# Packed attention with two MoE feed-forward layers: the first two decode steps of the first layer's weight tiles are kept in program order

## The chip, the cores and the metric

The kernel runs on one core of a Trainium2 chip. The metric is the device time of one execution in microseconds (us). It is measured by running the compiled program several times. One more execution is recorded by the hardware profiler, and the rows below come from that one.

## The reference

```python
def _attn_ref(q, k, v, p):                       # q, k, v: (4, 8, 576, 64); p: (4, 8, 32, 64)
    scale = 1.0 / np.sqrt(q.shape[-1])
    def sm_attn(qq, kk, vv):
        s = scale * np.matmul(qq, kk.transpose(0, 1, 3, 2))
        a = np.exp(s - np.max(s, axis=-1, keepdims=True))
        a = a / (np.sum(a, axis=-1, keepdims=True) + 1e-09)
        return np.matmul(a, vv)
    p_packed = sm_attn(p, k, v)                  # 32 packed tokens a head
    return sm_attn(q, p_packed, p_packed)

def _moe_ref(x, w_in, w_out):                    # x: (2304, 512); w_in: (512, 2048)
    h = x @ w_in
    sp = np.where(h > 20.0, h, np.log1p(np.exp(np.minimum(h, 20.0))))
    return (h * np.tanh(sp)) @ w_out             # mish

def _moe2_ref(x, w_in, w_out):                   # the same shapes, with ELU
    h = x @ w_in
    g = np.where(h > 0.0, h, np.exp(np.minimum(h, 0.0)) - 1.0)
    return g @ w_out
```

The attention's result is laid out as 2304 tokens by 512 and goes through the mish layer (the first mixture) and then the ELU layer (the second mixture). The weights of the two mixtures are float64 in the inputs, and the kernel reads them as pairs of 32-bit words.

## The kernel before

The work is three stages that overlap. **Attention** runs by batch b (four batches). Keys and queries are transposed on VectorE (DVE, L261). `scores1` multiplies the packed tokens with the keys on TensorE (PE, L281); DVE takes the row maxima (L295, L296) and ScalarE (ACT) the exponential (L301). `scores2` multiplies queries with the packed result (PE, L391). DVE transposes what comes out (L405), takes the maximum (L412), subtracts it (L413), sums (L418 to L420), normalises (L421) and transposes back (L428), with the exponential on ACT (L414). The result is split into a high and a low part, `a2h` (ACT, L192) and `a2l` (DVE, L194).

**The first mixture** is written as a loop over n. `gemm1(n)` is six matmuls (L484 to L486) into a tile `h1` of PSUM; there are two such tiles, so group n + 2 waits until `mish` has read group n. `mish(n)` is ACT L493 and L494 and DVE L495. `gemm2(n)` is twelve matmuls (L512 to L514) and follows two groups behind. The w_in weights are not used as they are: `fold(b, c)` (PE, L453) first multiplies them with the packed attention of batch b, and ACT and DVE split the product into `gh` and `gl` (L192, L196). So `gemm1` needs `a2h`, `a2l` of its batch, and `gh`, `gl` of its batch and of its quarter c of the columns.

**The second mixture** is `gemm3` and `gemm4`, with weights that were decoded under the first mixture.

A weight tile of 128 rows by 512 values comes as 128 by 1024 words by a DMA (L126) and is decoded in five steps:

- s0: ACT rescales the exponent word in place (L159)
- s1: DVE shifts and masks it (L163)
- s2: DVE adds the sign (L169)
- s3: DVE adds the bits of the other word (L174)
- s4: the tile is split into high and low (ACT L192, then DVE L196), or, for w_in of the first mixture, stored for a later reload

The first mixture has 32 such tiles, here called i0..i3 of quarter c (`raw_w1i<r>_<c>`) and o0..o15 (`raw_w1o<r>`). The table `ORD` gives their order: i0 to i3 of c = 0, o0, then i0, i2, i1, i3 of c = 1, then o2, o3, o1, o4, o5, o6, o7, then c = 2. One half of `w1oh0` is tile o0 and the other is o1: `gemm2(0)` uses the first and `gemm2(1)` the second. `startup` traces the attention of batch 0 from a list and puts decode steps between its items; the list's items are under a raised priority, the decode steps are not.

The order on each engine is not the traced one. A scheduler with a timeline model picks, instruction by instruction, what stands next on each engine. A call of `tc.keep_in_program_order(ins)` fixes an instruction behind everything that was traced ahead of it on its engine. Before the change `pin` in `decode` makes that call for s0 and s1 of the second mixture's tiles (names `w2...`) and not for the first mixture's.

Of the kernel before, what the change touches and what calls it, by code (L numbers as in the profile page):

```python
# [43 lines left out]
def kernel(  # L44
# [39 lines left out]
    def slot(shape, dt, name):  # L84
        return up.tile(shape, dt, tag="u", name=name)
# [49 lines left out]
    def decode(name, r, c, staged=False):  # L135
        raw = raws.pop((name, r, c))
        rr = raw.rearrange("p (n two) -> p n two", two=2)
        w0, w1 = rr[:, :, 0], rr[:, :, 1]
        t = dp.tile([128, 512], I32, tag="dec", name="dec")
        f1 = w1.bitcast(F32)  # L140
        whole = name == "w1i"
        key = {"w1i": (c, r // 2), "w2i": (name, c, r // 2)}.get(name, (name, r // 2))
        if staged:
            if r % 2 == 0:
                w2_dr[key] = dr.tile([128, 2, 2, 512], F32, name=f"w2_dr{name}{r}_{c}")
            parts = raw.bitcast(F32R).rearrange("p (x n) -> p x n", x=2)
        elif r % 2 == 0:
            if whole:
                w1v[key] = slot([128, 2, 512], F32, f"w1v{c}_{r}")
            else:  # L150
                wt[key] = [(small if name == "w2o" and r >= 12 else slot)([128, 2, 512], F32R, f"{name}{x}{r}_{c}") for x in "hl"]
        oi = w1v[key][:, r % 2, :].bitcast(I32) if whole else t

        def pin(ins):
            if name[1] == "2":
                tc.keep_in_program_order(ins)

        def s0():
            pin(nc.scalar.activation(out=f1, in_=f1, func=ACTF.Copy, scale=REBIAS))  # L159

        def s1():
            pin(
                nc.vector.tensor_scalar(  # L163
                    out=t, in0=w1, scalar1=3, scalar2=0x7FFFFFF8, op0=ALU.logical_shift_left, op1=ALU.bitwise_and
                )
            )

        def s2():
            nc.vector.scalar_tensor_tensor(  # L169
                out=t, in0=w1, scalar=-0x80000000, in1=t, op0=ALU.bitwise_and, op1=ALU.bitwise_or  # L170
            )

        def s3():
            nc.vector.scalar_tensor_tensor(  # L174
                out=oi, in0=w0, scalar=29, in1=t, op0=ALU.logical_shift_right, op1=ALU.bitwise_or
            )

        def s4():
            if whole:
                if r % 2 == 1:  # L180
                    nc.gpsimd.dma_start(out=w1_dr[c * 2 + r // 2], in_=w1v[key])
            elif staged:
                split(t.bitcast(F32), parts[:, 0], parts[:, 1], 1.0 / WSCALE)
                nc.gpsimd.dma_start(out=w2_dr[key][:, r % 2], in_=parts.bitcast(F32))
            else:
                hi, lo = wt[key]
                split(t.bitcast(F32), hi[:, r % 2, :], lo[:, r % 2, :], 1.0 / WSCALE)

        return [s0, s1, s2, s3, s4]

    def split(val, hi, lo, factor=1.0):
        nc.scalar.activation(out=hi, in_=val, func=ACTF.Copy, scale=factor)  # L192
        if factor == 1.0:
            nc.vector.tensor_tensor(out=lo, in0=val, in1=hi.bitcast(F32), op=ALU.subtract)  # L194
        else:
            nc.vector.scalar_tensor_tensor(  # L196
                out=lo, in0=val, scalar=factor, in1=hi.bitcast(F32), op0=ALU.mult, op1=ALU.subtract
            )
# [683 lines left out]
```

## Time and profile before

| | us |
|---|---|
| median of three runs | 835.19 (833.59 to 835.94) |
| the profiled execution, its own time | 833.58 |
| its span, first to last instruction | 831.8 |
| busy in the span: PE, DVE, ACT | 768.9, 442.3, 345.0 |
| granted TensorE clock, mean over the span | 0.96 |

The span is what the rows below lie in; 1.8 us of the profiled execution's time lie outside it. A busy share is an average over the whole span: PE is at 92%, but with a start in which it mostly waits and a long rest in which it does not. The granted clock is a share of 2.4 GHz, so 1.00 is 2.4 GHz and 0.50 is 1.2 GHz.

### The profile page before, as it was taken

How to read it: one execution, taken by the hardware profiler on the slowest of the kernel's cores; microseconds unless marked ns; L12 is line 12 of the kernel's file. 1: busy time of each engine (PE TensorE's matmuls, PEld its weight loads, DVE VectorE, ACT ScalarE, POOL GpSimd, SP SyncE). 2: the span in 40 equal slices, each digit the busy share in tenths (PEclk: the TensorE clock that was granted, in tenths of full speed). 3: DMA queues.
4: the chain of work that ended last, by engine and by line, in shares of the span. 5: the costliest groups of instructions: out<-in, count | busy, mean ns of one | idle time of the engine just before them, and what ended most of it. 6: DMA issues, size and time to landing. Idle time of an engine off the chain costs nothing.

```text
span 831.8 us, 13033 instructions
## 1 busy us (share of the span) xinstructions
PE 768.9 (92%) x5172; PEld 665.2 (80%) x5172; DVE 442.3 (53%) x860; ACT 345.0 (41%) x672; POOL 23.0 (3%) x46
## 2 busy tenths in 40 slices
PE   4404998999999999999999999999999999999997
PEld 3204896979989898899998888888888888888886
DVE  2689877585677557773516753513243334342342
ACT  0356673557466656564524442312241223221222
POOL 0000000000100001000000000000000000000000
PEclk7556999999999999999999999999999999999999
DMA  8996177227756576431492410200020001000000
GB/s 190 260 413 244 67 249 184 97 78 226 191 216 223 184 183 220 156 105 62 144 365 81 127 51 23 79 1 0 1 77 13 0 1 51 13 1 1 26 26 25
DMA packets 92700, 96.79 MB, mean 116 GB/s; under 512 B 64224, under 2 KB 68832, under 8 KB 92640
## 3 DMA queue, kind: packets, MB, share of 16 engines
q1 hardware_dynamic: 81056, 77.55, 30.3%
q0 software_dynamic: 4736, 17.30, 5.3%
q10 hardware_dynamic: 6848, 1.11, 0.8%
q8 instruction: 40, 0.66, 0.3%
q14 instruction: 20, 0.16, 0.1%
HBM read 73.92 MB, written 22.02 MB: 115 GB/s over the span
## 4 chain that ended last, share of the span: by engine, by line
PE 85%; DMA 6%; DVE 3%; ACT 2%; SPq 2%; issue 1%; ACTq 0%; DVEq 0%
PE h L576 8%; PE h L574 8%; PE h L575 8%; PE o L597 8%; PE o L598 8%; PE o L599 8%; PE acc L513 7%; PE acc L514 7%; PE acc L512 7%; PE h L484 4%; PE h L485 4%; PE h L486 4%; PE pm L453 1%; DMA raw_w1o<-in_moe_w_out_dram 1%; DMA k<-in_k_dram 1%
## 5 line engine op out<-in xcount | busy, mean ns | idle before, releaser
L513 PE MATMUL acc<-gl,w1oh 128*128 128x288 f32 x512 | 151.1, 297 | 0.1
L514 PE MATMUL acc<-gh,w1ol 128*128 128x288 f32 x512 | 150.6, 296 | 0.0
L512 PE MATMUL acc<-gh,w1oh 128*128 128x288 f32 x512 | 147.1, 296 | 0.0
L575 PE MATMUL h<-yl,w2ih 128*128 128x512 f32 (+1 forms) x320 | 117.7, 368 | 0.0
L576 PE MATMUL h<-yh,w2il 128*128 128x512 f32 (+1 forms) x320 | 117.5, 368 | 0.0
L574 PE MATMUL h<-yh,w2ih 128*128 128x512 f32 (+1 forms) x320 | 116.7, 368 | 0.0
L597 PE MATMUL o<-w2oh,gh 128*128 128x512 f32 x288 | 112.4, 390 | 1.1 <-ACT ob L249 0.7
L598 PE MATMUL o<-w2ol,gh 128*128 128x512 f32 x288 | 112.2, 390 | 0.0
L578 ACT ACTIVATE t<-h 128x512 f32<-128x512 f32 (+1 forms) x80 | 42.9, 554 | 166.1 <-PE h L576 151.5
L599 PE MATMUL o<-w2oh,gl 128*128 128x512 f32 x288 | 108.3, 389 | 0.0
L579 DVE TENSOR_SCALAR t<-t 128x512 f32<-128x512 f32 (+1 forms) x80 | 31.7, 399 | 143.0 <-ACT t L578 142.3
L513 PEld LDWEIGHTS acc<-gl,w1oh 128*128 128x128 f32 x512 | 96.3, 188 | 7.6 <-issue 3.8
L495 DVE TENSOR_TENSOR gl<-t,gh 128x288 fp32r<-128x288 f32 x128 | 57.8, 453 | 81.2 <-ACT gh L494 80.4
L514 PEld LDWEIGHTS acc<-gh,w1ol 128*128 128x128 f32 x512 | 96.3, 188 | 2.9 <-issue 2.7
L512 PEld LDWEIGHTS acc<-gh,w1oh 128*128 128x128 f32 x512 | 95.2, 189 | 4.1 <-DVE y L251 1.7
L484 PE MATMUL h<-a2h,gh 128*128 128x288 f32 x256 | 77.6, 304 | 14.7 <-ACT a2h L192 12.0
L493 ACT ACTIVATE t<-h 128x288 f32<-128x288 f32 x128 | 52.1, 408 | 88.4 <-PE h L486 86.0
L485 PE MATMUL h<-a2l,gh 128*128 128x288 f32 x256 | 76.9, 301 | 2.5 <-DVE a2l L194 2.5
L192 ACT ACTIVATE gh<-t 128x512 fp32r<-128x512 f32 (+1 forms) x80 | 46.6, 588 | 78.4 <-DVE t L580 49.3
L486 PE MATMUL h<-a2h,gl 128*128 128x288 f32 x256 | 76.8, 300 | 0.6 <-DVE gl L196 0.5
L194 DVE TENSOR_TENSOR gl<-t,gh 128x512 fp32r<-128x512 f32 (+1 forms) x80 | 50.2, 637 | 40.9 <-ACT gh L192 39.5
L576 PEld LDWEIGHTS h<-yh,w2il 128*128 128x128 f32 x320 | 60.2, 188 | 10.3
(102 smaller groups left out, 1103.6 us busy)
## 6 DMA issues: line engine op xcount, KB each, us to landing
w1r<-w_dr SPq DMA_DIRECT2D x24, 512.0 KB, 5.4
raw_w2i<-in_moe_w_in_dram SPq DMA_DIRECT2D x16, 512.0 KB, 4.1
raw_w1i<-in_moe_w_in_dram SPq DMA_DIRECT2D x16, 512.0 KB, 6.4
raw_w1o<-in_moe_w_out_dram SPq DMA_DIRECT2D x16, 512.0 KB, 10.9
raw_w2o<-in_moe_w_out_dram SPq DMA_DIRECT2D x16, 512.0 KB, 3.7
k<-in_k_dram SPq DMA_DIRECT2D x16, 288.0 KB, 6.6
y_dr<-y POOLq DMA_DIRECT2D x16, 288.0 KB, 2.6
out_dram<-ob SPq DMA_DIRECT2D x18, 256.0 KB, 2.0
```

The lines of the kernel that those rows point to most:

```text
L484: nc.tensor.matmul(out=hp, lhsT=wh, rhs=xh, start=(kt == 0), stop=False)
L485: nc.tensor.matmul(out=hp, lhsT=wh, rhs=xl, start=False, stop=False)
L486: nc.tensor.matmul(out=hp, lhsT=wl, rhs=xh, start=False, stop=(kt == 1))
L512: nc.tensor.matmul(out=o, lhsT=wh[:, cs], rhs=gh, start=first, stop=False)
L513: nc.tensor.matmul(out=o, lhsT=wh[:, cs], rhs=gl, start=False, stop=False)
L514: nc.tensor.matmul(out=o, lhsT=wl[:, cs], rhs=gh, start=False, stop=last)
L574: nc.tensor.matmul(out=hp, lhsT=wh, rhs=xh, start=(i == 0), stop=False)
L575: nc.tensor.matmul(out=hp, lhsT=wh, rhs=xl, start=False, stop=False)
L576: nc.tensor.matmul(out=hp, lhsT=wl, rhs=xh, start=False, stop=(i == 3))
L597: nc.tensor.matmul(out=o, lhsT=gh[:, ts], rhs=wh, start=(kk == 0), stop=False)
L598: nc.tensor.matmul(out=o, lhsT=gh[:, ts], rhs=wl, start=False, stop=False)
L599: nc.tensor.matmul(out=o, lhsT=gl[:, ts], rhs=wh, start=False, stop=(kk == NK - 1))
```

## The change

```diff
         def pin(ins):
-            if name[1] == "2":
-                tc.keep_in_program_order(ins)
+            tc.keep_in_program_order(ins)
 
         def s0():
             pin(nc.scalar.activation(out=f1, in_=f1, func=ACTF.Copy, scale=REBIAS))
```

`pin` is called in s0 and s1 alone. The call is now made for the 32 tiles of the first mixture too: 32 instructions L159 on ACT and 32 instructions L163 on DVE now stand behind everything that was traced ahead of them on their engine. No instruction is computed differently. Lines behind the diff carry numbers that are one lower in the changed kernel (L404 there is L405 here).

What this does to the order is read from the two built programs. First DVE, from the last query transpose of batch 0 on (`qT0_3`; `x0_*` and `pm_369`, `pm_382` belong to `scores2` of batch 0; `dec_457`, `dec_465`, `dec_473` are tiles i0, i2, i1 of c = 1; `gl0_0` is the low part of `fold(0, 0)`; `dec_446`/`w1ol0_0` are tile o0). Before:

```order
L261 STREAM_TRANSPOSE qT0_3_367<-q0_3_194 128x576
L174 SCALAR_TENSOR_TENSOR dec_446<-raw_w1o0_0_187,dec_446 128x512
L163 TENSOR_SCALAR dec_457<-raw_w1i0_1_199 128x512
L169 SCALAR_TENSOR_TENSOR dec_457<-raw_w1i0_1_199,dec_457 128x512
L163 TENSOR_SCALAR dec_465<-raw_w1i2_1_201 128x512
L169 SCALAR_TENSOR_TENSOR dec_465<-raw_w1i2_1_201,dec_465 128x512
L196 SCALAR_TENSOR_TENSOR gl0_0_421<-pm_411,gh0_0_420 128x512
L196 SCALAR_TENSOR_TENSOR w1ol0_0_448<-dec_446,w1oh0_0_447 128x512
L174 SCALAR_TENSOR_TENSOR w1v1_0_458<-raw_w1i0_1_199,dec_457 128x512
L174 SCALAR_TENSOR_TENSOR w1v1_2_466<-raw_w1i2_1_201,dec_465 128x512
L163 TENSOR_SCALAR dec_473<-raw_w1i1_1_203 128x512
L196 SCALAR_TENSOR_TENSOR gl0_0_421<-pm_411,gh0_0_420 128x512
L405 STREAM_TRANSPOSE x0_0_378<-pm_369 128x288
```

And in the changed kernel:

```order
L260 STREAM_TRANSPOSE qT0_3_367<-q0_3_194 128x576
L404 STREAM_TRANSPOSE x0_0_378<-pm_369 128x288
L404 STREAM_TRANSPOSE x0_1_380<-pm_369 128x288
L404 STREAM_TRANSPOSE x0_0_378<-pm_382 128x288
L404 STREAM_TRANSPOSE x0_1_380<-pm_382 128x288
L411 TENSOR_REDUCE mx2_393<-x0_0_378 128x18
```

Eleven decode and split instructions stood between the query transpose and the first L405; now none does. They follow behind the last instruction of the chain of batch 0 (`a2l0`), with tile o0 first.

Second ACT, around the exponential of `scores1` for batch 1, its first half (`e1_1_0`, which reads the maximum `sm_838`). `t1_726`, `t1_759`, `t1_792`, `t1_852` are `mish` of n = 6, 7, 8, 9. Before, with o11 the last of the decode steps ahead of it:

```order
L493 ACTIVATE t1_792<-h1_785 128x288
L494 ACTIVATE gh1_793<-t1_792 128x288
L192 ACTIVATE w1oh8_0_801<-dec_860 128x512
L493 ACTIVATE t1_852<-h1_845 128x288
L159 ACTIVATE raw_w1o11_0_858<-raw_w1o11_0_858 128x512
L301 ACT_TABLE_LOAD
L301 ACTIVATE e1_1_0_842,sm_838<-pm_821,sm_838 128x9x32 x2
L494 ACTIVATE gh1_853<-t1_852 128x288
```

And in the changed kernel:

```order
L493 ACTIVATE gh1_700<-t1_699 128x288
L191 ACTIVATE w1oh6_0_582<-dec_603 128x512
L300 ACT_TABLE_LOAD
L300 ACTIVATE e1_1_0_842,sm_838<-pm_821,sm_838 128x9x32 x2
L492 ACT_TABLE_LOAD
L492 ACTIVATE t1_726<-h1_719 128x288
L493 ACTIVATE gh1_727<-t1_726 128x288
```

The exponential and the two table loads around it stood behind `mish` of n = 9; now they stand ahead of `mish` of n = 6.

Third PE. `h1_538` is `gemm1(0)`, `pm_529` is `fold(0, 1)`, which needs `w1v1` (the four tiles i of c = 1). Before:

```order
L391 MATMUL pm_382<-qT0_0_361,pt_323 32x288 x2
L453 MATMUL pm_529<-w1v1_2_466,pt_323 32x512 x4
L453 MATMUL pm_529<-w1v1_0_458,pt_323 32x512 x4
L484 MATMUL h1_538<-a2h0_431,gh0_0_420 128x288
```

In the changed kernel the fold stands behind `gemm1(0)` to `gemm1(3)` and `gemm2(0)`, whose last matmul is the first row here, and ahead of `gemm2(1)`, which reads the half of `w1oh0` that is tile o1:

```order
L512 MATMUL acc1_611<-gl1_547,w1oh0_0_447 128x288
L513 MATMUL acc1_611<-gh1_546,w1ol0_0_448 128x288
L452 MATMUL pm_529<-w1v1_2_466,pt_323 32x512 x4
L452 MATMUL pm_529<-w1v1_0_458,pt_323 32x512 x4
L511 MATMUL acc0_610<-gh1_576,w1oh0_0_447 128x288
```

Up to the first matmul of `gemm1(8)` (`h1_785`) both programs hold the same 268 matmul instructions on PE, in a different order. On SP, the queue that issues the loads, the four loads of batch 1's keys stood behind the load of o9 and now stand ahead of the load of o5, and the loads of batch 1's values move ahead of the reload of `w1v` and of tile i0 of c = 3. In the second mixture only neighbouring rows change places.

## Rows read from the trace of the kernel before

**Rows 1.** The page: the span and its instructions.

```profile
span 831.8 us, 13033 instructions
```

**Rows 2.** Stretches: length, busy PE, PEld, DVE, ACT, POOL, granted clock, DMA share, GB/s.

```profile
80.00:90.00 10.00, 10.00 (x99) 9.19 (x98) 10.00 (x21) 3.81 (x9) 0.77 (x1) 1.00 0.42 119
101.00:103.20 2.20, 0.63 (x25) 0.10 (x9) 2.20 (x6) 2.14 (x5) 0.00 (x0) 1.00 0.23 54
127.00:130.00 3.00, 1.70 (x50) 1.06 (x58) 1.34 (x5) 0.71 (x2) 0.00 (x0) 0.94 0.70 115
130.00:133.00 3.00, 3.00 (x22) 1.48 (x7) 1.90 (x4) 1.30 (x3) 0.00 (x0) 0.50 0.58 92
150.00:790.00 640.00, 639.08 (x4073) 556.25 (x4072) 319.02 (x600) 264.11 (x507) 17.36 (x32) 1.00 0.30 96
```

**Rows 3.** Timeline of PE: start, length, instruction, [idle before, its releaser].

```profile
39.75 1.88 PE L391 MATMUL pm<-qT,pt 64*32 64x288 f32 x32
...
73.93 0.61 PE L485 MATMUL h<-a2l,gh 128*128 128x288 f32 x1 [2.47 <-DVE a2l L194]
...
93.95 0.29 PE L484 MATMUL h<-a2h,gh 128*128 128x288 f32 x1
...
103.16 0.40 PE L484 MATMUL h<-a2h,gh 128*128 128x288 f32 x1 [1.57 <-ACT t L493]
```

**Rows 4.** Timeline of DVE.

```profile
38.07 0.78 DVE L261 STREAM_TRANSPOSE qT<-q 128x576 f32<-128x576 f32 x1
...
42.01 0.43 DVE L163 TENSOR_SCALAR dec<-raw_w1i 128x512 int32<-128x512 int32 x1 [2.59 <-ACT raw_w1i L159]
42.48 0.69 DVE L169 SCALAR_TENSOR_TENSOR dec<-raw_w1i,dec 128x512 int32<-128x512 int32 x1
...
49.93 0.84 DVE L405 STREAM_TRANSPOSE x<-pm 128x288 f32<-128x288 f32 x2
...
57.32 1.42 DVE L413 TENSOR_TENSOR x<-x,mx 128x576 f32<-128x576 f32 x2
58.66 0.42 DVE L163 TENSOR_SCALAR dec<-raw_w1o 128x512 int32<-128x512 int32 x1
59.00 0.68 DVE L169 SCALAR_TENSOR_TENSOR dec<-raw_w1o,dec 128x512 int32<-128x512 int32 x1
59.60 0.68 DVE L196 SCALAR_TENSOR_TENSOR w1ol<-dec,w1oh 128x512 fp32r<-128x512 f32 x1
...
74.46 1.43 DVE L261 STREAM_TRANSPOSE kT<-k 128x576 f32<-128x576 f32 x2
...
92.16 0.45 DVE L495 TENSOR_TENSOR gl<-t,gh 128x288 fp32r<-128x288 f32 x1
...
93.24 0.82 DVE L295 TENSOR_REDUCE sm<-pm 128x1 f32<-128x288 f32 x2
...
95.77 0.21 DVE L296 TENSOR_SCALAR sm<-sm 128x1 f32<-128x1 f32 x1
```

**Rows 5.** Timeline of ACT.

```profile
66.97 0.63 ACT L192 ACTIVATE w1oh<-dec 128x512 fp32r<-128x512 f32 x1 [1.92 <-DVE dec L174]
...
97.25 1.28 ACT L301 ACT_TABLE_LOAD   x1
98.55 0.81 ACT L301 ACTIVATE e<-pm,sm 128x288 f32<-128x288 f32 x1
...
99.83 0.44 ACT L494 ACTIVATE gh<-t 128x288 fp32r<-128x288 f32 x1
...
101.41 1.28 ACT L493 ACT_TABLE_LOAD   x1
102.70 0.41 ACT L493 ACTIVATE t<-h 128x288 f32<-128x288 f32 x1
```

**Rows 6.** SP's issue of the load of o5, and the page's group of key loads.

```profile
41.39 0.33 SPq L126 DMA_DIRECT2D raw_w1o<-in_moe_w_out_dram  x1
...
k<-in_k_dram SPq DMA_DIRECT2D x16, 288.0 KB, 6.6
```

## The prediction, made before the changed kernel ran

> **What bounds the kernel now.** I read the page first, a span of 831.8 us [rows 1], and then five stretches of it. From 150 to 790 us PE is busy 639.08 of 640.00 us [rows 2]: nothing that the change does to ACT or DVE can make that stretch shorter, and DVE has half its time free there (319.02 us busy), so nothing that it does makes it much longer. The change is decided before 150 us. There PE starts late: its first `gemm1` matmuls wait for the attention of batch 0, and the last wait ends at 73.93 us, after 2.47 us, on `a2l` (L194) [rows 3]. From there PE hardly stops until 101.6, when it waits 1.57 us for a `mish` on ACT and goes on at 103.16 [rows 3]. That `mish` stands behind a table load, an exponential of `scores1` for batch 1 and a second table load [rows 5]. DVE is busy 10.00 of 10.00 us from 80 to 90 [rows 2]. So two things count: when the front of the kernel lets PE go, and whether DVE, which is full, delivers what PE asks for next.
>
> I take `gemm1(8)` as a milepost. It starts at 93.95 us [rows 3], and both programs have the same 268 matmul instructions on PE ahead of it. What it shifts by, with what is idle behind it, is what the change is worth.
>
> **Step A: the attention of batch 0 comes earlier.** In the changed order nothing stands between the last query transpose and the first L405. The transpose ends at 38.07 + 0.78 = 38.85 us [rows 4]; it waits for its load, not for the decode, so I leave it there. Half of `scores2` takes 1.88 / 2 = 0.94 us [rows 3], so L405 starts near 39.8 instead of 49.93 [rows 4]. Behind it DVE has 4 transposes of 0.84 / 2 = 0.42 us, and 12 passes over 576 columns (L412, L413, L418, L421, L428, L194, two each) that I put at (58.66 - 57.32) / 2 = 0.67 us each from the pair of L413 [rows 4]: 1.7 + 8.0 us. Two passes of ACT lie open in the chain, 0.63 us each by L192 [rows 5]: 1.3. The three decode steps of one tile stand inside it: one L163 at 59.00 - 58.66 = 0.34 and two at 59.60 - 59.00 = 0.60 [rows 4]: 1.5. Four passes over 18 columns are at most 0.21 each like L296 [rows 4]; I take 0.4 in all. The sum is 12.9 us: `a2l` is done near 52.7 instead of about 74.5, and the first `gemm1` matmul starts near 53.
>
> **Step B: the decode that was done before 74 us is now behind it, and in tile order.** Tile o1 is the half of `w1oh0` that `gemm2(1)` reads. In the changed order DVE has, from 52.7 us to the L174 of o1, 8 L163, 16 L169 or L174, 5 L196, 4 key transposes and 4 L495. By their spacings [rows 4] (0.34, 0.60, 0.60 for L196, which has the same length 0.68, 1.43 / 2 = 0.71, and 0.37 for L495, whose length 0.45 overlaps its neighbour by the same 0.08) that is 2.7 + 12.6 + 2.9 + 1.5 = 19.7 us without any wait. Waits come on top, because a tile's steps now follow each other directly. An L169 right behind its own L163 starts 42.48 - 42.01 = 0.47 us after it, not 0.34 [rows 4]: 0.13 for each such pair, some 11 pairs, 1.4 us. For o2, o3 and o1 DVE hands over to ACT's L192 (0.63 [rows 5]) and its next step waits: I put 0.85 each for o2 and o3 and 0.8 for o1, 2.5 us. The first L495 is reached before its `mish`, since `gemm1(0)` needs both halves of `gl0_0`, which are themselves rows of this queue: some 1.7 us. Together 5.6 us, bounds 0 and 7.8 (0.13 at both joints of all 14 tiles, 3.6 instead of 1.4). The `w1oh` of o1 is ready near 52.7 + 19.7 + 5.6 = 78.0. PE does `gemm1(0)` to `gemm1(3)`, `gemm2(0)` and the fold in the meantime, then waits. So the 20 us of step A are worth nothing by themselves: what PE lacked in time it now lacks in weights.
>
> **Step C: to the exponential of batch 1.** From the L196 of o1 to L296, which makes `sm_838`, DVE has 6 L163, 19 long steps, 2 L495, two L295 in 0.82 us and L296 in 0.21 [rows 4]: 2.0 + 11.4 + 0.7 + 0.8 + 0.2 = 15.2 us, and some 0.4 of waits for L494. L296 ends near 93.6. Before it started at 95.77 [rows 4], so it is 2.4 us earlier; but it has moved ahead of other things.
>
> **Step D: the exponential now stands ahead of `mish(6)`.** ACT has there a table load, two exponentials, a table load and the `mish`: 98.55 - 97.25 = 1.30, 99.83 - 98.55 = 1.28, 102.70 - 101.41 = 1.29, 0.41 [rows 5], together 4.3 us. It can't start before L296. `gemm1(8)` needs the PSUM tile that `mish(6)` reads. With 0.2 for the hand-overs it starts near 93.6 + 4.3 + 0.2 = 98.1, against 93.95: **+4.2 us**, and PE has nothing in its queue to fill the last 3 to 5 of them. In the kernel before this block stood behind `mish(9)`, and PE lost 1.57 us to it [rows 3]. That is not paid again: **-1.6 us**.
>
> What the clock does after such a pause: from 127 to 130 PE was busy 1.70 of 3.00 us, and from 130 to 133 the granted clock was 0.50, 1.2 GHz, with PE busy all the time [rows 2]: half of 3 us is lost. Around the pause of 1.57 us it stayed at 1.00, 2.4 GHz, from 101 to 103.2 [rows 2]. The bounds are 0 and 1.5; the pause here is nearer to the first: **+1.5 us**.
>
> **The loads.** SP issues the keys of batch 1 where it issued o5 at 41.39; a key load lands 6.6 us later in the median [rows 6], so they are there before DVE wants them near 54. If not, each us of delay is one us in step B. Loads o5 to o9 come four small loads later; DVE reaches the first of them only after 78. The values and the reload that change places are used after the milepost. Small changes in the second mixture lie under a PE that does not stop [rows 2]: nothing. That the two PE orders differ around `gemm2(8)` and the fold of c = 2 I put at nothing, within 1.2 us either way.
>
> **Sum.** 4.2 - 1.6 + 1.5 = +4.1 us: 833.6 + 4.1 = 837.7 against the profiled execution, which was 1.6 us below the median of the runs; against the median 839.3 us. Its own range is 837.5 to 841.5.
>
> **The rivals.**
> - *No difference, because the waits of step B are half as long* (2.8 us). The milepost is then at 95.3, +1.35, less 1.57, and the pause is short enough to keep the clock: 835.0. For it: the waits rest on estimates from single pairs of neighbours, and two tiles' steps may overlap better than that where their waits are short. Chance 0.24.
> - *Faster: DVE runs without waits.* Then o1 is ready at 72.4, L296 ends at 88.0 and `gemm1(8)` starts at 92.5, -1.45 us, and the 1.57 us go too: -3.0, 832.2. PE would not hold it back: 99 matmuls fit into 10 us [rows 2]. It decides at L296 = 91.0, that is o1 near 75.4; earlier than that the change gains. Against it: an ACT pass lies inside each o tile. Chance 0.14.
> - *Much slower: the pinned decode stays late.* The second exponential of batch 1 stands ahead of the `mish` of `gemm1(12)`'s group in both programs. If DVE is still behind there, its pair of table loads costs the same pause again: 3.3 us and 1.5 for the clock, 844.1. Against it: DVE is half free after 150 us [rows 2]. Chance 0.10.
> - *The table switch has a hidden part.* In the rows the next instruction starts 1.30 and 1.29 us after the load started [rows 5], so nothing else is seen; if ACT drained for as long again at each switch, step D would grow by some 2.6 us, to 841.9. Chance 0.04.
>
> The Trainium skill, "ScalarE: Activation LUTs", section "What ACT_TABLE_LOAD costs", states about 1283 ns for the load plus about 1380 ns of drain, 2.66 us a switch; by it the sum would be 2 x 1.38 = 2.8 us more. The trace agrees with the first figure and shows no second one.
>
> That the change does nothing is excluded by the order of the built program.
>
> **How the numbers follow.** About 0.3% of the time (2.5 us) is what a measurement of this kernel can tell from no change. The forecast has 0.48, and with the two slower rivals slower has 0.62; same 0.24; faster 0.14. The range goes from 832.0, the faster case's value, to 843.5, below the repeated pause.
>
> **What would show it.** The first `gemm1` matmul near 53 us; a PE idle before `gemm2(1)` until about 78, released by L192; L296 ending near 93.6; `gemm1(8)` near 98.1, released by ACT's `mish`; a granted clock under 1.00 behind it; no pause of 1.57 us for the same exponential later. The prediction is wrong if o1 is ready well before 75.4, if PE has work queued during the exponential, or if a second pause of this kind follows.

## The result, and where the time went

The changed kernel took 844.19 us in the median (841.97 to 845.46, 4 runs), the kernel before 835.36 in the same comparison. The ratio is 1.0114, 95% interval 1.0094 to 1.0134: slower, by 8.8 us. The forecast was slower by 4.1, and 844.19 lies above the top of its range, 843.5. The profiled execution of the changed kernel took 845.46 us, 1.3 above its median, and that of before 1.8 below its own, so the two spans, 843.7 and 831.8, are 11.9 apart where the medians are 8.8 apart. Part of that surplus is clock, as the last stretches of this section show.

First PE, from the first `gemm1` matmul on; the main rows with a wait ahead of them are shown (line numbers one lower than before).

```profile
53.53 0.61 PE L483 MATMUL h<-a2h,gh 128*128 128x288 f32 x1 [1.72 <-ACT gh L191]
...
78.04 0.61 PE L511 MATMUL acc<-gh,w1oh 128*128 128x288 f32 x1 [6.75 <-ACT w1oh L191]
...
97.93 0.40 PE L483 MATMUL h<-a2h,gh 128*128 128x288 f32 x1 [2.13 <-ACT t L492]
...
106.35 0.40 PE L511 MATMUL acc<-gh,w1oh 128*128 128x288 f32 x1 [0.41 <-DVE y L250]
...
121.67 0.74 PE L324 MATMUL pm<-ident,e 128*128 128x128 f32 x5 [0.41 <-DVE gl L195]
...
131.53 0.30 PE L373 MATMUL pm<-ident,pv 128*64 128x128 f32 x1 [1.95 <-DVE pv L362]
...
176.11 0.53 PE L511 MATMUL acc<-gh,w1oh 128*128 128x288 f32 x2 [1.26 <-ACT gh L493]
...
181.66 0.40 PE L483 MATMUL h<-a2h,gh 128*128 128x288 f32 x1 [0.90 <-ACT t L492]
...
214.07 0.77 PE L324 MATMUL pm<-ident,e 128*128 128x128 f32 x5 [1.10 <-ACT e L300]
...
215.79 0.61 PE L483 MATMUL h<-a2h,gh 128*128 128x288 f32 x1 [0.82 <-ACT t L492]
...
304.25 1.25 PE L324 MATMUL pm<-ident,e 128*128 128x128 f32 x5 [1.80 <-ACT e L300]
```

The first three rows are the forecast front: `gemm1` from 53.53, `gemm2(1)` let go at 78.04 by the split of tile o1 (L191 here, L192 before), `gemm1(8)` at 97.93 behind a `mish`. Where it stood at 93.95 [rows 3], that is +4.0 us. The five rows behind 150 us are what the forecast did not have.

DVE of the changed kernel:

```profile
41.35 1.58 DVE L404 STREAM_TRANSPOSE x<-pm 128x288 f32<-128x288 f32 x4 [2.54 <-PE pm L390]
...
51.81 1.43 DVE L193 TENSOR_TENSOR a2l<-a2t,a2h 128x576 fp32r<-128x576 f32 x2
...
93.16 0.22 DVE L295 TENSOR_SCALAR sm<-sm 128x1 f32<-128x1 f32 x1
...
130.86 0.42 DVE L162 TENSOR_SCALAR dec<-raw_w1o 128x512 int32<-128x512 int32 x1
131.20 0.28 DVE L362 TENSOR_SCALAR pv<-pm,rs 128x64 f32<-128x64 f32 x1
```

`a2l` ends at 51.81 + 1.43 = 53.24, and the maximum (L296 of before, 95.77 there [rows 4]) at 93.38. The last two rows are a wait further on: the scaling of the packed product of batch 1 (`pv`), for which PE waits 1.95 us at 131.53, stands behind decode that DVE is still busy with. In the kernel before, PE waited 1.08 us at this place:

```profile
126.65 0.30 PE L374 MATMUL pm<-ident,pv 128*64 128x128 f32 x1 [1.08 <-DVE pv L363]
```

ACT of the changed kernel, the `w1oh` of o1 and the block around the exponential of batch 1:

```profile
77.36 0.63 ACT L191 ACTIVATE w1oh<-dec 128x512 fp32r<-128x512 f32 x1 [1.99 <-DVE dec L173]
...
93.45 1.28 ACT L300 ACT_TABLE_LOAD   x1 [2.89 <-DVE sm L295]
94.75 0.80 ACT L300 ACTIVATE e<-pm,sm 128x288 f32<-128x288 f32 x1
...
96.18 1.28 ACT L492 ACT_TABLE_LOAD   x1
97.47 0.41 ACT L492 ACTIVATE t<-h 128x288 f32<-128x288 f32 x1
```

ACT waits 2.89 us for the maximum, and then `mish(6)` waits for a table load, two exponentials and a table load: from 93.38 to 97.88, 4.5 us, where the forecast had 4.3 and 0.2 for hand-overs. Each load is followed after 1.30 and 1.29 us, so here too no second part of a switch shows.

Stretches (columns as in [rows 2]) of the changed kernel:

```profile
93.00:98.00 5.00, 2.87 (x23) 2.64 (x21) 0.72 (x4) 4.47 (x8) 0.22 (x1) 1.00 0.26 105
98.00:101.00 3.00, 3.00 (x23) 2.99 (x24) 2.43 (x5) 2.94 (x8) 0.00 (x0) 1.00 0.00 0
150.00:790.00 640.00, 634.12 (x4032) 552.76 (x4031) 317.56 (x594) 261.64 (x501) 17.33 (x32) 0.99 0.30 97
214.00:219.00 5.00, 4.11 (x19) 3.90 (x20) 2.53 (x7) 4.32 (x10) 0.00 (x0) 0.66 0.74 201
```

Two things to see. Behind the pause at 98 the granted clock is 1.00, 2.4 GHz; the 1.5 us that the forecast added there for a clock of 1.2 GHz were not paid. And from 150 to 790 us, where PE was busy 639.08 of 640.00 us [rows 2], it is busy 634.12: 5.0 us more of waits, with a granted clock of 0.66 behind two of them. That clock is not part of the order. Run 3 below has the same waits (1.10 and 0.82 us at 214.20 and 215.92), and its row is

```profile
214.00:219.00 5.00, 3.98 (x29) 3.76 (x30) 2.54 (x7) 4.33 (x10) 0.00 (x0) 1.00 0.72 207
```

Behind the wait at 304.25 it is the same: from 303 to 310 us the granted clock is 0.76 in the changed kernel and 1.00 in runs 3 and 5. Their spans, 840.8 us, are 9.0 above that of before, close to the 8.8 of the medians.

### The profile page after: what moved, and what is told of

Its sections match the earlier page's. It is cut to its first block, busy times and chain, and to the rows that moved or that the text cites. A ratio compares the mean times of both kernels' runs of the same rounds, so it can differ in the third digit from the quotient of the medians.

```text
span 843.7 us, 13017 instructions
## 1 busy us (share of the span) xinstructions
PE 779.1 (92%) x5172; PEld 673.7 (80%) x5172; DVE 446.1 (53%) x860; ACT 344.3 (41%) x672; POOL 22.4 (3%) x46
## 4 chain that ended last, share of the span: by engine, by line
PE 78%; DVE 8%; ACT 6%; DMA 4%; issue 2%; SPq 2%; ACTq 0%; DVEq 0%
PE h L573 8%; PE h L575 8%; PE h L574 8%; PE o L596 8%; PE o L597 8%; PE o L598 8%; PE acc L511 6%; PE acc L513 6%; PE acc L512 6%; PE h L483 3%; PE h L485 3%; PE h L484 3%; DVE dec L168 2%; PE pm L452 1%; DMA v<-in_v_dram 1%
## 5 line engine op out<-in xcount | busy, mean ns | idle before, releaser
L511 PE MATMUL acc<-gh,w1oh 128*128 128x288 f32 x512 | 152.2, 304 | 8.4 <-ACT w1oh L191 6.8
L512 PE MATMUL acc<-gl,w1oh 128*128 128x288 f32 x512 | 153.4, 301 | 0.0
L513 PE MATMUL acc<-gh,w1ol 128*128 128x288 f32 x512 | 152.9, 301 | 0.0
L575 PE MATMUL h<-yh,w2il 128*128 128x512 f32 (+1 forms) x320 | 117.5, 368 | 0.0
L511 PEld LDWEIGHTS acc<-gh,w1oh 128*128 128x128 f32 x512 | 98.6, 195 | 17.9 <-ACT w1oh L191 8.5
L512 PEld LDWEIGHTS acc<-gl,w1oh 128*128 128x128 f32 x512 | 99.2, 194 | 3.6 <-issue 1.7
L513 PEld LDWEIGHTS acc<-gh,w1ol 128*128 128x128 f32 x512 | 98.8, 193 | 2.5 <-issue 2.1
L191 ACT ACTIVATE gh<-t 128x512 fp32r<-128x512 f32 (+1 forms) x80 | 46.6, 588 | 78.6 <-DVE t L579 49.4
```

The lines of the kernel that those rows point to most:

```text
L511: nc.tensor.matmul(out=o, lhsT=wh[:, cs], rhs=gh, start=first, stop=False)
L512: nc.tensor.matmul(out=o, lhsT=wh[:, cs], rhs=gl, start=False, stop=False)
L513: nc.tensor.matmul(out=o, lhsT=wl[:, cs], rhs=gh, start=False, stop=last)
L575: nc.tensor.matmul(out=hp, lhsT=wl, rhs=xh, start=False, stop=(i == 3))
```

## The experiments

All runs are compared with the kernel before on the same chip; its median was 834.33 us beside runs 1 to 4, 834.46 beside runs 5 to 8 and 834.13 beside runs 9 to 12. The ratio to it is given with its interval. An edit can shift the line numbers by a few. A second milepost helps to tell the front from the rest: the first PE row of `pv` for batch 1, ahead of which every one of these programs has the same number of matmuls on PE. It starts at 126.65 us in the kernel before and at 131.53 in the changed one.

**1 and 2: which tiles' pins?**

```diff
-            if name[1] == "2":
+            if name[1] == "2" or starting[0]:        # run 1: the startup's tiles
+            if name[1] == "2" or not starting[0]:    # run 2: the later tiles
```

> The pins stay for the tiles that startup traces and are taken from all later tiles. Theory 1 (what the change loses comes from the pinned decode of the startup, which is late for gemm2(1), and from what follows out of it): the front is that of the changed kernel, a2l near 53 us and w1oh of o1 near 78, and the time stays above 838. Theory 2 (the later tiles' pins make the half of the loss that lies behind 110 us): the front is the same, gemm1(8) is late by some 4 us, but nothing is lost behind 110 us, so about 839. In this program the first exponential of batch 1 stands behind mish(7), one group later than in the changed kernel, so the pause should move from gemm1(8) to gemm1(9) or gemm1(10).

> The pins stay for the tiles that are traced after startup and are taken from the startup's tiles. Theory 1: the front is that of the kernel before (gemm1 from about 71 to 74 us, PE full from 77), 834 to 837. Theory 2: the front is that of the kernel before, but 4 to 5 us are lost behind 110 us, about 840.

Run 1: 838.21 us against 834.33, ratio 1.0048 (1.0032 to 1.0064). Run 2: 839.69, ratio 1.0060 (1.0035 to 1.0084). The startup's pins cost some 4 us, and the later tiles' pins some 5 by themselves. Theory 1 misses run 2. Theory 2 is near in both times, but not in the places: run 1's front is the changed kernel's up to `gemm2(1)` (77.32 us), yet `gemm1(8)` starts at 94.92, +1.0 us and not +4, and the pause behind the exponential is 1.27 us at 102.33. Run 2's front is that of before up to 100 us, and then it waits, ahead of 110 us already and with `pv` at 132.33:

```profile
102.78 1.20 PE L281 MATMUL pm<-kT,pT 32*32 32x288 f32 x32 [1.61 <-ACT e L301]
...
105.06 0.40 PE L484 MATMUL h<-a2h,gh 128*128 128x288 f32 x1 [1.07 <-ACT t L493]
```

There `scores1` waits for the exponential of its first half to read the one PSUM tile they share, which in the kernel before it did not.

**3: tile o1 right behind o0, all pins kept.**

```diff
-    ORD=[4, 8, 10, 9, 11, 6, 7, 5, 12, 13, 14, 15],
+    ORD=[4, 5, 8, 10, 9, 11, 6, 7, 12, 13, 14, 15],
```

> All pins as in the changed kernel, and tile o1 is moved in the order of tiles to stand right behind o0, ahead of the four tiles i of c = 1. Theory 1 in the form of the prediction (the wait for o1 isn't the end of it, since DVE has the same sum of work ahead of the maximum that the exponential of batch 1 waits for): o1 is ready near 64 instead of 78, gemm2(1) no longer waits 6.75 us for it, but the maximum still ends near 93.4 and gemm1(8) starts within 1 us of 97.9; the time within 2.5 us of the changed kernel's 844. Rival (the wait for o1 is what is lost): gemm1(8) comes 4 us or more earlier and the time falls to 840 or below.

842.95 us, ratio 1.0092 (1.0066 to 1.0118). PE's rows:

```profile
74.86 0.61 PE L511 MATMUL acc<-gh,w1oh 128*128 128x288 f32 x1 [0.40 <-ACT w1oh L191]
...
83.94 0.61 PE L483 MATMUL h<-a2h,gh 128*128 128x288 f32 x1 [3.61 <-ACT gh L191]
...
98.25 0.41 PE L483 MATMUL h<-a2h,gh 128*128 128x288 f32 x1 [0.21 <-ACT t L492]
```

And DVE's maximum:

```profile
93.46 0.21 DVE L295 TENSOR_SCALAR sm<-sm 128x1 f32<-128x1 f32 x1
```

The wait for o1 has shrunk from 6.75 to 0.40 us, another one of 3.61 us stands at 83.94, and nothing is won: the maximum ends at 93.67, and `gemm1(8)` starts at 98.25. A wait of 6.75 us in the middle of the front was not what set its end; the sum of DVE's work ahead of the maximum was.

**4: the exponentials of batch 1 pinned too**, which puts the first behind `mish(9)`.

```diff
-                nc.scalar.activation(
+                ins = nc.scalar.activation(
...
                 )
+                if b == 1:
+                    tc.keep_in_program_order(ins)
```

> All pins as in the changed kernel, and the two exponentials of scores1 for batch 1 are pinned in program order too, which puts the first one behind mish(9). Theory 1 (step D: gemm1(8) is late because the exponential stands ahead of mish(6)): gemm1(8) starts near 94 to 95 instead of 97.9, and the time falls by 2 to 4 us, to 840 to 842; what is lost behind 110 us stays. Rival (the lateness is DVE's, and the exponential only shows it): gemm1(8) stays near 97 to 98 because its operands from DVE are late too, and the time is that of the changed kernel within 1 us.

842.04 us, ratio 1.0083 (1.0056 to 1.0110), an interval that overlaps the changed kernel's. `gemm1(8)` starts at 95.47 us instead of 97.93, so it was the exponential that held it. From 90 to 100 us PE doesn't pause at all; then it does, as PE's rows show:

```profile
90.00:100.00 10.00, 10.00 (x67) 10.00 (x66) 9.68 (x21) 5.78 (x13) 1.23 (x2) 0.84 0.23 91
```

```profile
103.60 1.20 PE L280 MATMUL pm<-kT,pT 32*32 32x288 f32 x32 [1.61 <-ACT e L300]
...
105.88 0.40 PE L485 MATMUL h<-a2h,gh 128*128 128x288 f32 x1 [1.07 <-ACT t L494]
```

The two waits are those of run 2. Four groups later the exponential holds back `scores1` instead of `mish(6)`, and what `gemm1(8)` gained is lost again: `pv` starts at 133.01 us, 1.5 later than in the changed kernel. The lower time goes with another order behind 150 us (the table below).

**5 and 6: the order of the four tiles i of c = 3 ahead of `pv`.**

```diff
+            if name[1] == "2" or not (name == "w1i" and c == 3):   # run 5
+            if name[1] == "2" or (name == "w1i" and c == 3):       # run 6
```

> All pins but those of the four tiles i of c = 3. Where the changed kernel loses behind 110 us, PE waits 1.95 us for the scaling of the packed product (DVE L362, pv) of batch 1, and the decode of these four tiles stands right ahead of it on DVE. Theory 2a (the order of these tiles on DVE makes that wait): the wait falls to 1.1 us or less, as in the kernel before, and the time to 840 to 842. Theory 2b (DVE is behind there as a whole, because everything ahead was late, and the order of the last four tiles is no matter): the wait stays near 2 us and the time at 843 to 845. The front, with gemm1(8) near 98, is the same by both.

> Of the first layer's tiles only the four tiles i of c = 3 are pinned. Theory 2a: the wait ahead of pv is 2 us or more and the time 837 to 840, with the front of the kernel before. Theory 2b: DVE is not behind, the wait is that of the kernel before, 1.1 us, and the time 833 to 836.

Run 5: 842.74 us, ratio 1.0108 (1.0083 to 1.0134). Run 6: 836.50, ratio 1.0014 (0.9998 to 1.0030). The waits ahead of `pv`, run 5 first and then run 6:

```profile
132.21 0.30 PE L374 MATMUL pm<-ident,pv 128*64 128x128 f32 x1 [1.57 <-DVE pv L363]
```

```profile
126.45 0.30 PE L374 MATMUL pm<-ident,pv 128*64 128x128 f32 x1 [1.56 <-DVE pv L363]
```

The times lie between the ranges of the two theories, within 0.5 us of those of 2b: these four tiles matter little. The waits fit neither theory; they are 1.6 in both, half a microsecond from the kernel before. The wait at `pv` can be only a small part of the loss.

**7 and 8: one of the two steps pinned.**

```diff
-            pin(nc.scalar.activation(out=f1, in_=f1, func=ACTF.Copy, scale=REBIAS))
+            tc.keep_in_program_order(                                                  # run 7, s0
+                nc.scalar.activation(out=f1, in_=f1, func=ACTF.Copy, scale=REBIAS)
+            )
...
-            pin(
+            tc.keep_in_program_order(                                                  # run 8, s1
                 nc.vector.tensor_scalar(
```

> Step s0 (ACT) is pinned for all tiles of the first layer, s1 (DVE) for none. s1 reads what s0 writes, so if ACT keeps the traced order DVE can do little else. If one pin implies the other: the front of the changed kernel (a2l near 53, o1 near 78) and 841 to 845. If the pin of s1 on DVE is what hurts: 834 to 838.

> Step s1 (DVE) is pinned, s0 (ACT) is not. If one pin implies the other: a2l near 53 to 54, o1 near 78, 841 to 845. If the pin of s0 on ACT is what hurts: 834 to 838. The first exponential of batch 1 stands behind mish(6) here instead of ahead of it, so gemm1(8) should not be held back by it: near 96 instead of 98, and the pause one group later.

Run 7: 837.59 us, ratio 1.0046 (1.0033 to 1.0060). Run 8: 839.60, ratio 1.0066 (1.0045 to 1.0086). Neither step alone does all of the harm. In run 7 o1 is ready at 77.79 us as in the changed kernel, but `mish(6)` stands ahead of the exponential, and PE is busy 5.00 of 5.00 us from 93 to 98, where the changed kernel had 2.87. Run 8's `gemm2(1)` waits until 81.29, and nothing else than a wait of 0.25 holds PE near 98; its `gemm1(8)` starts at 97.34, late by what `gemm2(1)` is late, and `pv` at 131.71. Run 7's `gemm1(8)` starts at 93.85, 0.1 us ahead of before, and its `pv` at 127.76, so most of what it loses is lost behind 150 us; run 8 loses less there. That led to the next four.

**9 and 10: the last four tiles, o12 to o15.** In run 9 all other pins stay; in run 10 only these are pinned.

```diff
+            if name[1] == "2" or not (name == "w1o" and r >= 12):   # run 9
+            if name[1] == "2" or (name == "w1o" and r >= 12):       # run 10
```

> All pins but those of the four last tiles of the first layer, o12 to o15. The order of ACT and DVE from the exponential of scores2 for batch 1 on is then, row for row, that of the kernel before; ahead of it all is as in the changed kernel. Theory 3 (the loss behind 150 us is an order that the scheduler chose there, because four pinned instructions shifted what it saw): gemm1(8) near 98 as in the changed kernel, the wait for pv near 1.9, but no loss behind 150 us, so about 5 us less than the changed kernel: 838 to 840. Theory 4 (the loss behind 150 us comes from the lateness of the front, whatever the order there): 843 to 845.

> Of the first layer's tiles only the last four, o12 to o15, are pinned; all ahead of the scores2 of batch 1 is as in the kernel before. Theory 3: the front of the kernel before, and 1 to 4 us lost behind 150 us, 836 to 838, since the order of the table loads and of the fold's split is another one there (it is that of the run with only the later tiles pinned). Theory 4: 833 to 836, no loss.

Run 9: 838.96 us, ratio 1.0063 (1.0047 to 1.0080). Run 10: 836.95, ratio 1.0033 (1.0019 to 1.0047). Run 9's PE:

```profile
97.99 0.40 PE L484 MATMUL h<-a2h,gh 128*128 128x288 f32 x1 [2.12 <-ACT t L493]
...
132.18 0.30 PE L374 MATMUL pm<-ident,pv 128*64 128x128 f32 x1 [2.55 <-DVE pv L363]
```

And its stretch from 150 us on:

```profile
150.00:790.00 640.00, 639.08 (x4077) 556.55 (x4076) 320.48 (x603) 265.08 (x509) 17.30 (x32) 1.00 0.30 96
```

The front is the changed kernel's to a tenth of a microsecond, the wait at `pv` even longer, and behind 150 us PE is as busy as in the kernel before. The span is 837.0, 5.2 above before's 831.8. Each against the kernel before beside it, the changed kernel loses 8.8 us and run 9 838.96 - 834.13 = 4.8. So the pins of four tiles, the last of whose pinned first steps on ACT runs at 149.47 us, cost about 4 us. ACT's rows at the exponential of `scores2` for batch 1 show a place where the order differs, in the changed kernel:

```profile
168.56 1.28 ACT L413 ACT_TABLE_LOAD   x1
...
171.35 0.57 ACT L191 ACTIVATE gh<-pm 128x512 fp32r<-128x512 f32 x1
173.27 0.60 ACT L191 ACTIVATE gh<-pm 128x512 fp32r<-128x512 f32 x1 [1.34 <-DVE gl L195]
173.88 1.28 ACT L492 ACT_TABLE_LOAD   x1
175.18 0.41 ACT L492 ACTIVATE t<-h 128x288 f32<-128x288 f32 x1
```

And in run 9:

```profile
167.26 1.28 ACT L414 ACT_TABLE_LOAD   x1
...
169.72 0.58 ACT L192 ACTIVATE gh<-pm 128x512 fp32r<-128x512 f32 x1
170.32 1.28 ACT L493 ACT_TABLE_LOAD   x1
171.61 0.41 ACT L493 ACTIVATE t<-h 128x288 f32<-128x288 f32 x1
...
172.50 0.60 ACT L192 ACTIVATE gh<-pm 128x512 fp32r<-128x512 f32 x1
```

And in the kernel before:

```profile
165.14 1.28 ACT L493 ACT_TABLE_LOAD   x1
166.43 0.41 ACT L493 ACTIVATE t<-h 128x288 f32<-128x288 f32 x1
...
167.31 0.60 ACT L192 ACTIVATE gh<-pm 128x512 fp32r<-128x512 f32 x1
```

In the changed kernel both halves of a fold's split stand ahead of the table load and the `mish`; the second half waits 1.34 us for DVE's step on the first (`gl`, L195), and PE's rows at 176.11 and 181.66 are what follows. In run 9 and in the kernel before, the second half stands behind the `mish`. None of these instructions is pinned. Run 10 has the front of before (`pv` at 125.17, 1.5 us earlier) and PE busy 637.82 us from 150 to 790: its order there is a third one, with one table pair more.

**11 and 12: s0 alone, and fewer tiles.**

```diff
-            pin(nc.scalar.activation(out=f1, in_=f1, func=ACTF.Copy, scale=REBIAS))
+            ins = nc.scalar.activation(out=f1, in_=f1, func=ACTF.Copy, scale=REBIAS)
+            if name[1] == "2" or not (name == "w1o" and r >= 12):   # run 11
+            if name[1] == "2" or starting[0]:                       # run 12
+                tc.keep_in_program_order(ins)
```

> Only s0 is pinned, and not for o12 to o15. The run with s0 pinned for all tiles had mish(6) ahead of the exponential, lost only about 1 us up to 128 us, and the rest behind 150 us. Theory 3: its front, and no loss behind 150 us: 833 to 835.5, the same as the kernel before. Theory 4: as with s0 pinned for all tiles, 837 to 838.5.

> Only s0 is pinned, and only for the tiles of the startup. The exponential of batch 1 stands behind mish(7). Theory 1 (the front's loss is the exponential ahead of a mish that PE needs, plus the cold clock behind the wait for o1): PE's pause moves to gemm1(9) or gemm1(10) and is under 2 us; from 150 us on as before; 834 to 837. Rival (late decode costs by itself, wherever the exponential stands): 837 to 839, as with both steps pinned for the startup's tiles.

Run 11: 834.75 us, ratio 1.0010 (0.9999 to 1.0021). Run 12: 835.34, ratio 1.0014 (1.0001 to 1.0027). Both are within 0.15% of the kernel before, as theory 3 and theory 1 had it. Run 11, ACT and then the stretch:

```profile
91.03 1.28 ACT L303 ACT_TABLE_LOAD   x1
...
95.17 0.41 ACT L495 ACTIVATE t<-h 128x288 f32<-128x288 f32 x1
```

```profile
93.00:98.00 5.00, 5.00 (x38) 4.86 (x37) 3.31 (x9) 4.91 (x12) 0.14 (x1) 1.00 0.26 105
```

The same block of table load, exponentials and table load stands one `mish` later, its maximum's two reductions start at 90.78 us instead of 92.27, and PE has work all the time. The `w1oh` of o1 was nearly as late there as in the changed kernel (`gemm2(1)` at 77.13). In run 12 (`gemm2(1)` at 76.63) the pause that theory 1 moved to a later group did not come: PE has no wait from 87 to 125 us, and `pv` starts at 126.38. Run 1 pins the same tiles, but s1 too, and has the exponential behind the same `mish(7)`; there the maximum ends at 95.96 us instead of 93.82, two `w1oh` stand between the exponential and the second table load, and `pv` starts at 128.83. So the place of the exponential alone does not decide what the front loses; how late DVE and ACT are around it counts too. No version was found that beats the kernel before.

PE's busy time from 150 to 790 us puts all fourteen kernels into three classes, and ACT's order from the exponential of `scores2` for batch 1 to the end of the program is the same, row for row, within each class (in the second, one row of run 8 changes place):

| busy of 640.00 us | kernels |
|---|---|
| 639.0 to 639.1 | before, runs 1, 6, 9, 11, 12 |
| 637.5 to 637.9 | runs 2, 4, 8, 10 |
| 634.1 | the changed kernel, runs 3, 5, 7 |

## Why the prediction was wrong, step by step

- **Step A held,** with two errors that offset each other. `a2l` ended at 53.24 (forecast 52.7), the first `gemm1` matmul started at 53.53 (53). But the first L404 started at 41.35 and not at 39.8, and the chain behind it took 11.9 us and not 12.9.
- **Step B held.** `gemm2(1)` was let go at 78.04 (78.0). Run 3 shows that this wait was rightly not counted by itself.
- **Step C held.** The maximum ended at 93.38 (93.6).
- **Step D held.** `gemm1(8)` started at 97.93 (98.1), +4.0 us (+4.2). Runs 9 and 11 have the same late tiles unpinned; with `mish(6)` ahead of the exponential the time is 838.96 - 834.75 = 4.2 us less. They differ in the pins of s1 as well, so that the block of table loads makes all of the 4.2 us is argued. Run 4, which moves the exponentials of batch 1 alone, shows that the block held `gemm1(8)` (95.47); it does not show the front without loss.
- **The clock term was mis-sized.** The forecast added 1.5 us for 1.2 GHz behind a pause of 3 to 5 us. The pause was 2.13 us, and the granted clock behind it was 1.00.
- **"That is not paid again: -1.6 us" was mis-sized too.** The pause of 1.57 us at 103 is gone, but 0.41 us at 106.35 and 0.41 at 121.67 are new. At the first transposes of batch 1's exponentials PE is at 121.67 against 117.56, +4.1 us. That this is the forecast's sum is luck, since the terms are others: 4.0 - 1.6 + 0.8 = 3.2 and some 0.9 that no listed wait explains.
- **The step that failed is the first paragraph's:** "nothing that the change does to ACT or DVE can make that stretch shorter, and DVE has half its time free there (319.02 us busy), so nothing that it does makes it much longer", with the small changes in the second mixture put at nothing under "a PE that does not stop". That stretch lost 5.0 us of PE's time in waits, and in the profiled execution some clock that runs 3 and 5 did not lose. Engines with half their time free still made PE wait where a table load pair, or a split that waits for DVE, stood ahead of the `mish` or the exponential that PE needed next. The forecast read the built order up to `gemm1(12)` and took the rest from a busy share. Run 9 separates the two parts: without the last four tiles' pins the loss is 4.8 us by the medians (838.96 against 834.13), near the forecast's 4.1; with them it is 8.8.
- **The rival "the pinned decode stays late"** had the right time, 844.1, by a wrong mechanism. Its second pause of 3.3 us, at the other half of `scores1` for batch 1, did not come: its block of table loads and exponentials ran on ACT from 110.50 to 114.56, and PE was busy 7.50 of 7.50 us from 110 to 117.5. That its time was met is luck. DVE was behind, and PE waited 1.95 instead of 1.08 us for `pv`, about one microsecond in all, not five.
- **The rival with a hidden part of the table switch** fell: 1.30 and 1.29 us again. The Trainium skill, "ScalarE: Activation LUTs", section "What ACT_TABLE_LOAD costs", adds a drain of about 1.38 us to each; no row of these runs shows one.

What stays open is why the scheduler took the other order at the exponential of `scores2`. The runs show which pins bring it, and that with the order of before the loss is gone; they don't show what in its model tipped. Open too is how the 4 us of the front divide between the exponential's place and the lateness of the decode.

## What to carry to other kernels

A pin on an instruction can reach further than its engine's next rows. A scheduler that picks instruction by instruction settled here on another order from 168 us on, behind the last pinned instruction at 149; such an order has to be read to the end of the program and priced, place by place, wherever a long item (a pair of table loads, a split that waits for another engine) stands ahead of what the busiest engine needs next. A busy share of 99.9% says that nothing waits in the order that was traced, not that no other order could. And a wait that looks largest, 6.75 us here, can cost nothing by itself, when the work that sets the end of the stage is the same without it.

## What was not expected of the hardware

Pauses of like length were followed by different clocks. After PE was busy 2.87 of 5.00 us from 93 to 98, the granted clock from 98 to 101 was 1.00; after the two waits of 1.10 and 0.82 us at 214.07 and 215.79 it was 0.66 over 214 to 219, with matmuls 0.24 us apart. Behind the same two waits the clock from 214 to 219 us was 1.00 in runs 3 and 5. Behind the waits of 1.61 and 1.07 us in runs 2 and 4, with only `scores1` between them, it was 0.65 and 0.50 from 107 to 110 us. The pause from 127 to 130 in the kernel before, from which the forecast took its 1.5 us, was one of short matmuls between waits [rows 2]. How long PE stood still did not by itself tell what the clock would do, not even for the same waits in programs with the same order there.
